# Sorted-block attention and a token/channel MLP on one core: plain second product in three batches, block products in the last, other slots for the token layer

## The chip, the core and the metric

The kernel runs on one NeuronCore of a Trainium2 chip. Five engines work side by side, each in its own program order: TensorE (PE, matmuls into PSUM), VectorE (DVE), ScalarE (ACT), GpSimd (POOL) and SyncE (SP, which here only starts transfers). Sixteen DMA engines move data. The metric is the time of one execution on the device in microseconds; lower is better. Inputs and output lie in the device's main memory in float32.

## The reference

Attention over sorted blocks, then a token-mixing layer and a feed-forward layer (FFN). Cut to what matters:

```python
# q, k, v: (4, 8, 768, 64); sort_net: (4, 8, 8, 8); blocks of 96 rows
P = sort_net
for _ in range(5):                       # row and column normalisation
    P = exp(P - P.max(-1)); P = P / P.sum(-1); P = P / P.sum(-2)
k_sorted = einsum('bhij,bhjcd->bhicd', P, k_blocks)
v_sorted = einsum('bhij,bhjcd->bhicd', P, v_blocks)
attn = softmax(q_blocks @ k_sorted.T / sqrt(64)) @ v_sorted   # within a block
x = attn.transpose(0, 2, 1, 3).reshape(4, 768, 512)
a1 = alpha1 * x + beta1
u  = x + lam * einsum('ts,bsd->btd', w_tok, a1)               # token layer
a2 = alpha2 * u + beta2
out = u + lam * (relu(a2 @ w_ch1) @ w_ch2)                    # w_ch1 512 x 2048, w_ch2 2048 x 512
```

## The kernel before

Everything runs in one program, with the order of each engine written out by hand. After a start of some 36 us (sorting weights, batch 0's attention, weights loaded) the body is a walk over four batches b and, in each, three pairs g of token tiles (128 tokens each, so 256 per pair). For each pair (b, g) come:

- eight h units ("h", 0 to 7; `h_unit`): 8 matmuls of 256 columns each into a PSUM tile h_ps, 64 in a pair; ScalarE applies relu into hT (`h_part`).
- the product steps ("c", n): the second FFN product of the pair, from hT and W2p.

The work of the next batch is hung into numbered places of this walk: `put(b, g, kind, n, ...)` files it, `run` emits it right after h unit or product step n of pair (b, g). So a place sets where an instruction stands in the order of every engine that it uses, TensorE, VectorE, ScalarE, and the queues of SP and POOL.

Two forms of the second product exist. `ch_plain` (line 842): for each of the two token tiles, 16 matmuls of 512 columns into one PSUM tile ch_ps, four per step, eight steps; then VectorE multiplies by lam while it empties the PSUM tile, POOL adds u, SP stores. `ch_step` (line 787), the block form: the product is cut into 2 x 2 blocks and made with seven block products instead of eight (`product`), 7 x 8 = 56 matmuls of 256 columns into cha_ps and chb_ps. It needs four sums of blocks of hT per pair (`sums`, tile hs, eight VectorE operations), differences of blocks of W2p made once (`weights`, tiles T23 and T4, and one block of W2p overwritten), and several copies and adds on ScalarE and VectorE to put the four result blocks together. Before, pair (0, 0) is plain and the eleven others are in block form; the weight differences are made in pairs (0, 0) and (0, 1).

The hung-in work of batch b, in the pairs of batch b - 1 and the first ones of b:

- `load_kv`, `load_q`: POOL starts the loads of v, k (tile raw) and q (tile qn). The load of batch 3 is behind `gate` (line 201), a POOL copy that reads one element of uT of pair (1, 1), so it waits until that transposition has landed.
- `mix_matrix` (the sorting matrix spread over partitions, VectorE), `mix_v` and `mix_k` (matmuls that sort v and k; the results leave PSUM as mixed and kT), `bounce_v` and `back_v` (SP writes mixed to device memory, vscr, and reads it back in the layout of the tile Vs).
- q is turned: for batch 1 by TensorE (`q_turn_late`, line 511, qt_ps to qT), for batches 2 and 3 by transposing transfers of SP (`q_cross`).
- `score` (sc_ps, then exp on ScalarE) and `pv` (value products x_ps, then VectorE divides into x), 8 each per batch, through two PSUM slots psA that mix_ps and kmix_ps use too.
- `half_done` (line 953): VectorE moves tails of x between partitions and makes a half of a1, the operand a of the token layer.
- `moe_tok`: the token layer of one token tile, six matmuls of 512 columns into tok_ps; VectorE makes u from it, ScalarE a float16 copy. `moe_cross`: two transposing transfers of SP make uT of a pair. `moe_affine`: four VectorE operations make a2T, the input of the pair's h units.

h_ps, tok_ps, ch_ps, cha_ps, chb_ps and qt_ps go in turn through four PSUM slots (psB): a tile waits until the fourth tile before it has been emptied. Of u there are seven tiles, of ost (the output of a token tile) two.

Line 69 is the helper that records every engine instruction, so groups in the profile are told apart by their tiles.

Of the kernel before, what the change touches and what calls it, by code (L numbers as in the profile page):

```python
# [7 lines left out]
FT = mybir.dt.float32  # L8
F16 = mybir.dt.float16
BF = mybir.dt.bfloat16  # L10
AF = mybir.ActivationFunctionType
ALU = mybir.AluOpType
# [4 lines left out]
def kernel(  # L17
# [22 lines left out]
    B, H, S, D = q.shape  # L40
    NB = sort_net.shape[-1]
    BLK = S // NB
    C = H * D
    HID = moe_w_ch1.shape[1]
    NT = S // 128
    CT = C // 128
    HT = HID // 128
    BH = B * H
    HB = BLK // 2
    H4 = H // 2  # L50
    GRP = D + 2
    TAIL = 6 * BLK
    NG = NT // 2
    GS = 256
    HP = HT // 2
# [21 lines left out]
    pe = Engine(nc.tensor)  # L77
    dve = Engine(nc.vector)
    act = Engine(nc.scalar)
# [14 lines left out]
    def psb(shape, dtype, name):  # L94
        return pools["psB"].tile(shape, dtype, name=name, tag="psB")
# [92 lines left out]
    qn_of = {}  # L188

    gate = const([1, 1], F16, "gate")  # L190

    def load_q(b):
        qn_of[b] = att.tile([128, NT, H, D], F16, name="qn", tag="qn", bufs=1)
        for kt in range(NT):
            pool.dma_start(
                qn_of[b][:, kt, :, :], q[b, :, kt * 128:(kt + 1) * 128, :].rearrange("h p d -> p h d"),
            )
# [171 lines left out]
    def mix_matrix(b):  # L369
        mix_values(b, psa)  # L370
        big = att.tile([128, 2, H * NB], F16, name="bigM", tag="bigM", bufs=3)
        dve.tensor_tensor(
            big[:], bigV[b][:].rearrange("p h i -> p (h i)").unsqueeze(1).to_broadcast([128, 2, H * NB]),
            mth[:].unsqueeze(2).to_broadcast([128, 2, H * NB]), ALU.mult,
        )
        bigM[b] = big
        bgp = att.tile([128, 2, 2, H4, NB], F16, name="bigP", tag="bigP", bufs=3)
        for th in range(2):
            dve.tensor_tensor(
                bgp[:, :, th, :, :], bigV[b][:].rearrange("p (g a) i -> p a g i", a=2),  # L380
                mth[:, th:th + 1].unsqueeze(2).unsqueeze(3).to_broadcast([128, 2, H4, NB]), ALU.mult,
            )
        bigP[b] = bgp
# [127 lines left out]
    def q_turn_late(b, g, eng):  # L511
        if g == 0:
            qT_of[b] = att.tile([128, H4, S], F16, name="qT", tag="qT", bufs=1)
        ps = psb([128, S], F16, "qt_ps")
        for kt in range(NT):
            pe.transpose(
                ps[:, kt * 128:(kt + 1) * 128],
                qn_of[b][:, kt, 2 * g:2 * g + 2, :].rearrange("p a d -> p (a d)"), ident16[:],
            )
        eng(qT_of[b][:, g, :], ps[:])  # L520

    mixed = {}

# [161 lines left out]
    def moe_tok(b, kt, ps):  # L685
        tok_part(b, kt, 0, C, ps)
        if b not in u16_of:
            u16_of[b] = moep.tile([128, NT, C], F16, name="u16", tag="u16", bufs=1)
        u = u_tile(b, kt)
        dve.scalar_tensor_tensor(u, tok_of[(b, kt)][:], 1.0 / LIFT, x_of[b][:, kt, :], op0=ALU.mult, op1=ALU.add)  # L690
        act.copy(u16_of[b][:, kt, :], u)

    def moe_cross(b, g):
        uT = uT_of[(b, g)] = att.tile([128, CT, GS], F16, name="uT", tag="uT", bufs=2)
        for m in range(2):
            sp.dma_start_transpose(
                uT[:, :, m * 128:(m + 1) * 128], u16_of[b][:, 2 * g + m, :],
            )

    def moe_affine(b, g):  # L700
        for ci in range(CT):
            affine(b, g, ci, uT_of[(b, g)][:, ci, :], dve)
# [26 lines left out]
    def block(b, g, r, c):  # L729
        return hT_of[(b, g)][:, :, c, r * 128:(r + 1) * 128]  # L730
# [16 lines left out]
    def weights(n):  # L747
        B = [[W2p[:, r * HP:(r + 1) * HP, c * CH:(c + 1) * CH] for c in range(2)] for r in range(2)]
        if n == 0:
            T23.append(moep.tile([128, 2, HP, CH], F16, name="T23", tag="t23", bufs=1))  # L750
            T4.append(moep.tile([128, HP, CH], F16, name="T4", tag="t4", bufs=1))
            dve.tensor_tensor(T23[0][:, 1], B[1][1], B[0][1], ALU.subtract)
        elif n == 1:
            dve.tensor_tensor(T23[0][:, 0], T23[0][:, 1], B[0][0], ALU.add)
        elif n == 2:
            dve.tensor_tensor(T4[0][:], B[1][0], T23[0][:, 0], ALU.subtract)
        else:
            dve.tensor_tensor(B[0][1], B[0][1], B[0][0], ALU.subtract)
# [20 lines left out]
    def store(b, kt, ost, c, tail_q):  # L779
        sp.dma_start(out[b, kt * 96:(kt + 1) * 96, c], ost[0:96, c])  # L780
        tail_q(out[b, TAIL + kt * 32:TAIL + (kt + 1) * 32, c], ost[96:128, c])
# [59 lines left out]

    def ch_plain(b, g, n):
        kt = 2 * g + n // 4
        if n % 4 == 0:
            ch_of[0] = psb([128, C], FT, "ch_ps")
        cps = ch_of[0]
        for m in range(4 * (n % 4), 4 * (n % 4) + 4):
            pe.matmul(
                cps[:], block(b, g, n // 4, m // HP)[:, m % HP, :], W2p[:, m, :],
                start=(m == 0), stop=(m == HT - 1),  # L850
            )
        if n % 4 == 3:
            ost = att.tile([128, C], FT, name="ost", tag="ost", bufs=2)
            dve.tensor_tensor(ost[:], cps[:], lamB[:], ALU.mult)
            pool.tensor_tensor(ost[:], ost[:], u_of[(b, kt)][:], ALU.add)
            store(b, kt, ost, all_c, act_out)

    copy = dve.tensor_copy

# [64 lines left out]
    def put(b, hf, kind, n, *todo):  # L924
        at.setdefault((b, hf, kind, n), []).extend(todo)
# [17 lines left out]
    put(0, 0, "c", 3, lambda: moe_tok(0, 5, psb), lambda: moe_cross(0, 2))  # L943
    put(0, 0, "c", 5, lambda: moe_affine(0, 1))
    put(0, 1, "c", 1, lambda: moe_affine(0, 2))
    for n, at_ in enumerate(((0, "c", 7), (1, "h", 0), (1, "h", 1), (1, "h", 2))):
        put(0, *at_, lambda n=n: weights(n))
    put(1, 0, "h", 4, lambda: mix_matrix(3))

    def attn(b, kind, n):  # L950
        return (lambda: score(b, n // 2, n % 2, psa)) if kind == "s" else (lambda: pv(b, n // 2, n % 2))
# [25 lines left out]
    for b in range(1, B):  # L977
        p = b - 1
        if b > 1:
            for n, at_ in enumerate(((2, "h", 1), (2, "h", 3), (2, "h", 5))):  # L980
                put(p - 1, *at_, lambda b=b, n=n: mix_v(b, n, act.copy))
            put(p - 1, 2, "h", 7, lambda b=b: bounce_v(b))
            put(p - 1, 2, "c", 6, lambda b=b: back_v(b))
            for n in range(3):
                at_ = ((p - 1, 2, "c", 4), (p - 1, 2, "c", 6), (p, 0, "h", 1)) if b == 2 else (
                    (p - 1, 1, "c", 6), (p - 1, 2, "c", 4), (p - 1, 2, "c", 6)
                )
                put(*at_[n], lambda b=b, n=n: mix_k(b, n, (both[n == 2],) * 4))
            for kt in range(NT):
                at_ = (1, "c", 1) if b == 3 else (2, "h", 0) if kt < 3 else (2, "c", 0)  # L990
                put(p - 1, *at_, lambda b=b, kt=kt: q_cross(b, kt))
            if b + 1 < B:
                put(p, 0, "c", 0, lambda b=b: load_kv(b + 1), lambda b=b: load_q(b + 1))
            for what, at_ in (
                ("s0", (0, "h", 5)), ("s2", (0, "c", 1)), ("p0", (0, "c", 3)), ("s4", (0, "c", 5)), ("p2", (1, "h", 1)),
                ("s6", (1, "h", 3)), ("p4", (1, "c", 1)), ("p6", (1, "c", 3)),
            ):
                for i in range(2):
                    put(p, at_[0], at_[1], at_[2] + (i if what == "p6" else 0), attn(b, what[0], int(what[1]) + i))
            put(p, 1, "h", 2, half_done(b, 0))  # L1000
        put(p, *((1, "c", 6) if b == 1 else (2, "h", 0)), half_done(b, 1))
        put(p, 2, "h", 5, lambda b=b: moe_tok(b, 0, psb))
        put(p, 2, "h", 6, lambda b=b: moe_tok(b, 1, psb), lambda b=b: moe_cross(b, 0))
        put(p, 2, "c", 4, lambda b=b: moe_affine(b, 0))
        put(b, 0, "h", 0, lambda b=b: moe_tok(b, 2, psb))
        put(b, 0, "h", 2, lambda b=b: moe_tok(b, 3, psb), lambda b=b: moe_cross(b, 1))
        put(b, 0, "h", 5, lambda b=b: moe_tok(b, 4, psb))
        put(b, 0, "h", 7, lambda b=b: moe_tok(b, 5, psb), lambda b=b: moe_cross(b, 2))
        put(b, 0, "c", 4, lambda b=b: moe_affine(b, 1))
        put(b, 1, "c", 2, lambda b=b: moe_affine(b, 2))  # L1010

# [12 lines left out]
    for b in range(B):  # L1024
        for g in range(NG):
            for j in range(HP):
                if b or g or j > 2:
                    h_unit(b, g, j)
                    if j == 4 and (b or g):
                        sums(b, g, 0, 4, range(4))  # L1030
                    run(b, g, "h", j)
            for n in range(7 if b or g else 8):
                (ch_step if b or g else ch_plain)(b, g, n)
                run(b, g, "c", n)


# [28 lines left out]
```

## Time and profile before

| | |
|---|---|
| time, median of 13 runs | 271.24 us (269.39 to 276.16) |
| the profiled execution | 272.33 us, its span 270.5 us |
| mean granted clock of TensorE | 0.982 |
| matmuls of the h units | 768 of 128 x 256 |
| block products cha_ps, chb_ps | 352 and 264 of 128 x 256, in eleven pairs |
| plain product ch_ps | 32 of 128 x 512, in pair (0, 0) |
| VectorE hs (sums of blocks) | 44 + 22 + 22 operations, 0.42 us each |
| ScalarE copies out of cha_ps | 33 of 0.372 us |
| POOL ost + u | 22 of 1.336 us |
| Vs read back (Vs<-vscr) | 3 transfers, 7.8 to 9.0 us to landing |
| uT transpositions | 22, median 2.5 us to landing, longest 11.7 |
| loads of q (qn) | 18 of 128 KB, median 12.6 us to landing |

How to read it: a line of the timeline is a merged run of equal instructions with its start, the time from its first start to its last end, and, in brackets, how long the engine had stood idle before and what ended that. The recorded durations of matmuls overlap, so the pace of TensorE is read from starts. The DMA row of the page shows the transfer engines busy without a break from about 7 to 88 us, and little used after 150.

### The profile page before, as it was taken

What the parts mean: (1) busy time and instruction counts of PE and PEld (TensorE: products, weight loads), DVE (VectorE), ACT (ScalarE), POOL (GpSimd) and SP (SyncE); (2) the same over time, 40 slices, a digit from 0 to 9 for tenths busy, and PEclk for the clock granted to TensorE, in tenths of its full rate; (3) what the DMA queues carried; (4) which work ended last, traced back from release to release, by engine and by line L of the source; (5) the groups of instructions that cost most, each with busy time, mean ns of one, the idle gap of its engine ahead of it and who ended that gap; (6) DMA issues with size and microseconds to landing.
All of it is one profiled execution on the core that took longest, in us unless ns stands there. A gap on an engine that the chain in (4) does not pass through costs nothing.

```text
span 270.5 us, 6546 instructions
## 1 busy us (share of the span) xinstructions
PE 250.4 (93%) x2665; PEld 191.1 (71%) x2665; DVE 190.3 (70%) x433; ACT 147.5 (55%) x264; POOL 77.8 (29%) x94
## 2 busy tenths in 40 slices
PE   7986999999699889999999999999997999999992
PEld 3464776547488648767888678678896687788881
DVE  5768667779759945774989957647899574545554
ACT  3666575158654734948563956575725325444440
POOL 8791953314620300306610303001103020030300
PEclk9999999999889979999999999999999999999997
DMA  6999999999999265696999224970202104210202
GB/s 102 194 208 196 206 207 214 190 208 162 188 195 61 57 97 117 159 137 109 190 172 140 79 52 122 157 91 10 80 2 78 39 10 109 42 52 29 64 22 72
DMA packets 68078, 31.25 MB, mean 116 GB/s; under 512 B 57216, under 2 KB 63888, under 8 KB 68048
## 3 DMA queue, kind: packets, MB, share of 16 engines
q0 software_dynamic: 26352, 15.34, 43.0%
q1 hardware_dynamic: 41504, 15.36, 31.6%
q8 instruction: 21, 0.34, 0.5%
q10 hardware_dynamic: 192, 0.13, 0.2%
q14 instruction: 9, 0.07, 0.1%
HBM read 32.78 MB, written 8.65 MB: 153 GB/s over the span
## 4 chain that ended last, share of the span: by engine, by line
PE 58%; DVE 21%; DMA 9%; issue 4%; ACT 4%; POOL 2%; SPq 1%; ACTq 0%; DVEq 0%; POOLq 0%
PE h_ps L69 18%; PE cha_ps L69 11%; PE tok_ps L69 10%; PE chb_ps L69 8%; DVE ost L69 6%; DVE a L69 4%; DVE x L69 4%; DMA Vs<-vscr 3%; DMA v<-in_v_dram 3%; PE x_ps L69 3%; DVE kT L69 2%; DMA out_dram<-ost 2%; PE sc_ps L69 2%; PE v_ps L69 2%; DVE a2T L69 1%
## 5 line engine op out<-in xcount | busy, mean ns | idle before, releaser
L69 PE MATMUL h_ps<-a2T,W1p 128*128 128x256 bf16 x768 | 94.8, 276 | 0.5 <-DVE a2T L69 0.3
L69 PEld LDWEIGHTS <-W1p 128*128 128x128 bf16 x768 | 74.8, 99 | 14.8 <-issue 1.3
L69 ACT ACTIVATE hT<-h_ps 128x512 f16<-128x512 f32 x96 | 55.9, 601 | 26.8 <-PE h_ps L69 22.6
L69 POOL TENSOR_TENSOR ost<-ost,u 128x512 f32<-128x512 f32 x22 | 29.3, 1336 | 143.0 <-DVE ost L69 113.3
L69 PEld LDWEIGHTS <-hs 128*128 128x128 f16 x352 | 33.5, 98 | 4.9 <-issue 0.4
L69 PE MATMUL tok_ps<-a,w_tokT 128*128 128x512 f16 x132 | 32.6, 383 | 4.2 <-DVE a L69 4.1
L69 ACT CAST u<-u 128x512 f16<-128x512 f32 x22 | 13.6, 619 | 37.3 <-DVE u L69 37.3
L69 PEld LDWEIGHTS <-hT 128*128 128x128 f16 x296 | 28.1, 98 | 7.3 <-ACT hT L69 0.7
L69 DVE SCALAR_TENSOR_TENSOR u<-tok_ps,x 128x512 f32<-128x512 f32 x22 | 15.2, 692 | 21.7 <-PE tok_ps L69 18.9
L69 DVE TENSOR_TENSOR hs<-hT 128x512 f16<-128x512 f16 x44 | 18.5, 420 | 16.3 <-ACT hT L69 16.3
L69 ACT ACTIVATE et<-sc_ps 96x768 f16<-96x768 f32 (+1 forms) x32 | 24.8, 808 | 7.9 <-PE sc_ps L69 7.9
L69 PEld LDWEIGHTS <-w_tokT 128*128 128x128 f16 x132 | 12.8, 99 | 16.8 <-DVE a L69 5.0
L69 ACT COPY ost<-cha_ps 128x256 f32<-128x256 f32 x33 | 12.3, 372 | 22.2 <-PE cha_ps L69 19.6
L69 PE MATMUL cha_ps<-T,hs 128*128 128x256 f16 x176 | 22.8, 272 | 0.1
L69 PE MATMUL chb_ps<-W2p,hs 128*128 128x256 f16 x176 | 22.8, 273 | 0.0
L69 POOL DMA_DIRECT2D qn<-in_q_dram x18 | 16.0, 909 | 14.2 <-DMA raw<-in_v_dram 7.2
L69 ACT CAST kT<-kmix_ps 64x512 f16<-64x512 f32 x24 | 17.3, 720 | 3.0 <-PE kmix_ps L69 2.7
L69 DVE TENSOR_TENSOR ost<-ost,lamB 128x256 f32<-128x256 f32 (+1 forms) x23 | 18.3, 796 | 0.4
L69 PE MATMUL x_ps<-Vs,et 96*128 96x65 f16 (+4 forms) x288 | 13.4, 196 | 4.2 <-DMA Vs<-vscr 2.7
L69 DVE TENSOR_TENSOR ost<-ost,chb_ps 128x256 f32<-128x256 f32 x22 | 9.2, 418 | 11.3 <-PE chb_ps L69 10.4
L69 DVE TENSOR_TENSOR x<-x_ps,rcb 96x512 f16<-96x512 f32 x24 | 16.5, 686 | 0.8
L69 PEld LDWEIGHTS <-et 96*128 96x128 f16 (+4 forms) x288 | 12.4, 101 | 6.0 <-issue 4.0
(131 smaller groups left out, 323.5 us busy)
## 6 DMA issues: line engine op xcount, KB each, us to landing
out_dram<-ost SPq DMA_DIRECT2D x22, 192.0 KB, 2.2
raw<-in_v_dram POOLq DMA_DIRECT2D x6, 384.0 KB, 8.4
raw<-in_k_dram POOLq DMA_DIRECT2D x6, 384.0 KB, 11.8
qn<-in_q_dram POOLq DMA_DIRECT2D x18, 128.0 KB, 12.6
vscr<-mixed SPq DMA_DIRECT2D x6, 384.0 KB, 5.3
Vs<-vscr SPq DMA_DIRECT2D x3, 768.0 KB, 8.4
W1p<-in_moe_w_ch_dram POOLq DMA_DIRECT2D x4, 512.0 KB, 13.6
W2p<-in_moe_w_ch_dram POOLq DMA_DIRECT2D x4, 512.0 KB, 14.1
```

What stands on the lines that cost most here:

```text
L69: ins = getattr(self.eng, name)(*args, **kwargs)
```

## The change

1. A pair is in block form only in the last batch (`by_blocks`): pairs (0, 1) to (2, 2) use the plain form. The weight differences move from pairs (0, 0) and (0, 1) to pair (2, 2). `mix_matrix(3)` moves from pair (1, 0) to pair (0, 0).
2. The q of batch 1 is loaded in four transfers instead of six, in which a partition gets six rows that follow each other (1536 bytes in device memory); TensorE turns it with 12 transposes of 64 columns per two heads instead of 6 of 128, and the copy out of PSUM writes with a stride of six elements.
3. The token tiles of a batch move: of the six, the first two one h unit later, the third and fourth from pair (b, 0) to product steps 4 and 5 of the pair before, the last two to h units 2 and 3 of pair (b, 0). Their transposing transfers move with them.
4. The last value products move: p4 and p5 from product step 1 to h unit 6 of the second pair, p6 and p7 one product step earlier.
5. `ch_plain` gets a branch for the last token tile of all; with `by_blocks` as it is, it is not reached.

```diff
     def load_q(b):
+        if b == 1:
+            qn_of[b] = att.tile([128, H, NT, D], F16, name="qn", tag="qn", bufs=1)
+            for g in range(H4):
+                pool.dma_start(
+                    qn_of[b][:, 2 * g:2 * g + 2, :, :],
+                    q[b, 2 * g:2 * g + 2].rearrange("h (p t) d -> p h t d", t=NT),
+                )
+            return
...
         ps = psb([128, S], F16, "qt_ps")
-        for kt in range(NT):
-            pe.transpose(
-                ps[:, kt * 128:(kt + 1) * 128],
-                qn_of[b][:, kt, 2 * g:2 * g + 2, :].rearrange("p a d -> p (a d)"), ident16[:],
-            )
-        eng(qT_of[b][:, g, :], ps[:])
+        for t in range(NT):
+            for h2 in range(2):
+                pe.transpose(
+                    ps[h2 * 64:h2 * 64 + 64, t * 128:(t + 1) * 128], qn_of[b][:, 2 * g + h2, t, :], ident16[:],
+                )
+        eng(
+            qT_of[b][:, g, :].rearrange("p (r t) -> p r t", t=NT),
+            ps[:].rearrange("p (t r) -> p r t", t=NT),
+        )
...
+    def by_blocks(b, g):
+        return b == B - 1
...
-    for n, at_ in enumerate(((0, "c", 7), (1, "h", 0), (1, "h", 1), (1, "h", 2))):
-        put(0, *at_, lambda n=n: weights(n))
-    put(1, 0, "h", 4, lambda: mix_matrix(3))
+    for n, at_ in enumerate(((2, 2, "h", 3), (2, 2, "h", 5), (2, 2, "c", 2), (2, 2, "c", 7))):
+        put(*at_, lambda n=n: weights(n))
+    put(0, 0, "c", 7, lambda: mix_matrix(3))
...
-                ("s6", (1, "h", 3)), ("p4", (1, "c", 1)), ("p6", (1, "c", 3)),
+                ("s6", (1, "h", 3)), ("p4", (1, "h", 6)), ("p6", (1, "c", 2)),
...
-        put(p, 2, "h", 5, lambda b=b: moe_tok(b, 0, psb))
-        put(p, 2, "h", 6, lambda b=b: moe_tok(b, 1, psb), lambda b=b: moe_cross(b, 0))
-        put(p, 2, "c", 4, lambda b=b: moe_affine(b, 0))
-        put(b, 0, "h", 0, lambda b=b: moe_tok(b, 2, psb))
-        put(b, 0, "h", 2, lambda b=b: moe_tok(b, 3, psb), lambda b=b: moe_cross(b, 1))
-        put(b, 0, "h", 5, lambda b=b: moe_tok(b, 4, psb))
-        put(b, 0, "h", 7, lambda b=b: moe_tok(b, 5, psb), lambda b=b: moe_cross(b, 2))
+        put(p, 2, "h", 6, lambda b=b: moe_tok(b, 0, psb))
+        put(p, 2, "h", 7, lambda b=b: moe_tok(b, 1, psb), lambda b=b: moe_cross(b, 0))
+        put(p, 2, "c", 4, lambda b=b: moe_affine(b, 0), lambda b=b: moe_tok(b, 2, psb))
+        put(p, 2, "c", 5, lambda b=b: moe_tok(b, 3, psb), lambda b=b: moe_cross(b, 1))
+        put(b, 0, "h", 2, lambda b=b: moe_tok(b, 4, psb))
+        put(b, 0, "h", 3, lambda b=b: moe_tok(b, 5, psb), lambda b=b: moe_cross(b, 2))
...
-                    if j == 4 and (b or g):
+                    if j == 4 and by_blocks(b, g):
                         sums(b, g, 0, 4, range(4))
...
-            for n in range(7 if b or g else 8):
-                (ch_step if b or g else ch_plain)(b, g, n)
+            for n in range(7 if by_blocks(b, g) else 8):
+                (ch_step if by_blocks(b, g) else ch_plain)(b, g, n)
```

More of the change, by code (lines that the diff above doesn't have):

```diff
@@ L843, in ch_plain @@
         kt = 2 * g + n // 4
+        split = (b, kt) == (B - 1, NT - 1)
         if n % 4 == 0:
@@ L848, in ch_plain @@
             pe.matmul(
-                cps[:], block(b, g, n // 4, m // HP)[:, m % HP, :], W2p[:, m, :],
-                start=(m == 0), stop=(m == HT - 1),
-            )
-        if n % 4 == 3:
+                cps[:, lo_c if split else all_c], block(b, g, n // 4, m // HP)[:, m % HP, :],
+                W2p[:, m, lo_c if split else all_c], start=(m == 0), stop=(m == HT - 1),
+            )
+        if n % 4 < 3:
+            return
+        if not split:
             ost = att.tile([128, C], FT, name="ost", tag="ost", bufs=2)
             dve.tensor_tensor(ost[:], cps[:], lamB[:], ALU.mult)
-            pool.tensor_tensor(ost[:], ost[:], u_of[(b, kt)][:], ALU.add)
+            (dve if (b, g) == (B - 1, NG - 1) else pool).tensor_tensor(ost[:], ost[:], u_of[(b, kt)][:], ALU.add)
             store(b, kt, ost, all_c, act_out)
+            return
+        for c in (lo_c, hi_c):
+            if c is hi_c:
+                cps = psb([128, C], FT, "ch_ps")
+                for m in range(HT):
+                    pe.matmul(
+                        cps[:, c], block(b, g, 1, m // HP)[:, m % HP, :], W2p[:, m, c],
+                        start=(m == 0), stop=(m == HT - 1),
+                    )
+            ost = att.tile([128, C], FT, name="ost", tag="ost", bufs=2)
+            dve.tensor_tensor(ost[:, c], cps[:, c], lamB[:, c], ALU.mult)
+            dve.tensor_tensor(ost[:, c], ost[:, c], u_of[(b, kt)][:, c], ALU.add)
+            store(b, kt, ost, c, act.dma_start)
+    def by_blocks(b, g):
+        return b == B - 1
     copy = dve.tensor_copy
```

## The prediction

> **What bounds the kernel now.** I read the page first: busy shares, the clock row, the chain that ended last.
>
> ```profile
> span 270.5 us, 6546 instructions
> ...
> PE 250.4 (93%) x2665; PEld 191.1 (71%) x2665; DVE 190.3 (70%) x433; ACT 147.5 (55%) x264; POOL 77.8 (29%) x94
> ...
> PEclk9999999999889979999999999999999999999997
> ...
> PE 58%; DVE 21%; DMA 9%; issue 4%; ACT 4%; POOL 2%; SPq 1%; ACTq 0%; DVEq 0%; POOLq 0%
> ```
>
> TensorE is busy nearly always, and its clock dips near slices 11 and 14. Next the timeline of TensorE, for the price of a matmul and every wait in brackets.
>
> ```profile
> 50.90 1.02 PE L69 MATMUL ch_ps<-W2p,hT 128*128 128x512 f16 x4
> 51.76 1.46 PE L69 MATMUL tok_ps<-a,w_tokT 128*128 128x512 f16 x6
> ...
> 68.94 1.05 PE L69 MATMUL h_ps<-a2T,W1p 128*128 128x256 bf16 x8
> 72.68 0.44 PE L69 MATMUL x_ps<-Vs,et 96*128 96x65 f16 x8 [2.70 <-DMA Vs<-vscr]
> ...
> 73.48 1.89 PE L69 MATMUL h_ps<-a2T,W1p 128*128 128x256 bf16 x8
> ...
> 95.88 1.85 PE L69 MATMUL tok_ps<-a,w_tokT 128*128 128x512 f16 x6 [2.17 <-DVE a L69]
> ...
> 98.37 1.91 PE L69 MATMUL h_ps<-a2T,W1p 128*128 128x256 bf16 x8
> ...
> 209.39 1.47 PE L69 MATMUL tok_ps<-a,w_tokT 128*128 128x512 f16 x6 [1.64 <-DVE a L69]
> ...
> 238.58 7.15 PE L69 MATMUL h_ps<-a2T,W1p 128*128 128x256 bf16 x64
> 245.57 0.93 PE L69 MATMUL cha_ps<-W2p,hT 128*128 128x256 f16 x7
> ...
> 251.80 7.15 PE L69 MATMUL h_ps<-a2T,W1p 128*128 128x256 bf16 x64
> ```
>
> Starts give the true price, since durations overlap. 64 matmuls of 256 columns take 245.57 - 238.58 = 6.99 us, 0.109 each. Four of 512 columns take 51.76 - 50.90 = 0.86, 0.2157 each. A block pair takes 251.80 - 245.57 = 6.23 for 56 matmuls. There are three real waits (start to start 2.86, 2.33, 1.80), and after the first two come matmuls at half speed (eight in about 1.8 instead of 0.87): the granted clock is 0.5 for 3.41 us from 73.5 and from 97.4, costing 1.7 each. After the wait at 209 it stays at 1.0. Summing, over the matmuls from 36 us on, the distance to the next start less the median of its shape gives 20.2 us of loss. VectorE is what keeps TensorE waiting twice:
>
> ```profile
> 85.75 0.96 DVE L69 TENSOR_TENSOR a<-x,alphaB 128x1536 f16<-128x1536 f16 x1
> ...
> 91.97 1.86 DVE L69 COPY x<-x 32x512 f16<-32x512 f16 x3
> 93.87 0.96 DVE L69 TENSOR_TENSOR a<-x,alphaB 128x1536 f16<-128x1536 f16 x1
> ```
>
> The second half of the token operand comes behind some 3 us of output sums.
>
> **The change part by part.** *Plain product.* Eight pairs, (0,1) to (2,2), go from 56 matmuls of 256 columns to 32 of 512: 32 x 0.2157 = 6.90 against 56 x 0.109 = 6.10, +0.80 each, **+6.4**. Certain, since TensorE sets the pace there.
>
> *What the block form cost besides columns.* In the product stages of those eight pairs the same start-to-start sum loses 1.11, 0.27, 0.45, 0.51, 0.27, 0.45, 0.06 and 0.27 = 3.4 us on sums not ready and slots not free. A plain pair waits only for the last hT, which has 7 x 0.2157 = 1.5 us for a 0.60 activation. I leave 0.1 per pair: **-2.6**. VectorE sheds, per pair, eight sums of 0.42 and five or six output operations (0.4 to 0.9), and gains two evictions of 0.68: about 5 us. ScalarE sheds four copies of 0.37.
>
> *The token wait of batch 3* (1.80 at 207.6). Its operand is made at the head of pair (2,2): eviction 0.7, tails 0.9 to 1.9, two products 0.96, so 3.6 to 4.6 after the last product matmul. The token matmuls now follow seven h units (6.1) instead of six. Gone, as is batch 2's at 153.5 (0.5): **-2.3**. The weight differences (1.2, 2.2, 1.2 and 1.2 on VectorE) come behind it in pair (2,2), where VectorE otherwise has only evictions; batch 3 reads them some 15 us later.
>
> *The token wait of batch 1.* I walk the queues of pair (0,1) from the first value product. TensorE, with h 0.873, product step 0.863, value product 0.25, scores 0.28: the fourth h unit of pair (0,2) could start at 15.9, its token matmuls at 20.3. VectorE: the sixth x ends at 8.9; then half_done 2.8, eviction 0.6, two x of 0.84, half_done 2.8, and only then the eviction of the second product tile, done at 17.5. psB has four slots, and that fourth h unit takes the one of this tile. So the wait does not vanish: it becomes one for ch_ps, about 1.5 (0 if I overstate VectorE, 2.5 if the tails take 1.86 again): **-0.8**. At 1.5 it is shorter than the 1.80 that left the clock alone: **-1.7**.
>
> *The value wait* (2.86 at 69.8). Vs<-vscr is issued at 63.58 behind two transposes (1.2 each) and an output store whose issue took 1.9 while the 6144 short packets of q of batch 1 were draining (to 60.5). With 1024 long ones instead they should end near 56, estimated from the rate of the 1024-byte packets (195 per us). Store, transposes and bounce then go up to 1.5 earlier. TensorE arrives about 0.5 later, since the copy of q through VectorE writes with a stride. Bounds: wait 0.9 to 2.9; I take 1.2, **-1.7**, and the slow clock goes with it, **-1.7**. If SP gains nothing, both stay.
>
> *q by six-row runs.* 48 transposes of half width replace 24. No row shows a half-width transpose of 128 rows. Below: nothing, as six matmuls into separate column strips (rr_ps) took 0.40 where one takes 0.28; above: 24 x 0.056 = 1.3. Two strided copies on VectorE cost up to 0.4 more each. I take **+0.4**, being nearer to rr_ps.
>
> *Token layer in other slots.* Six tiles as before, none added. Two now use psB beside the product tile; they and kT of ScalarE leave hT 0.8 us of room. On SP the second pair of transposes now goes ahead of Vs<-vscr. Vs of batch 2 is issued some 13.4 us after the product of pair (0,2) begins; its first reader comes at 25.0; uncontended it takes 7.8. But see the slower rival: **+0.5**. The small waits of the h stages of (1,0) and (2,0), 1.02 and 0.70, lose their VectorE half: **-0.7**.
>
> Sum: 6.4 - 2.6 - 2.3 - 0.8 - 1.7 - 1.7 - 1.7 + 0.4 + 0.5 - 0.7 = **-4.2 us**. The profiled execution is 272.33 (span 270.5), 1.09 above the median of 271.24; from the median that gives **267.0**.
>
> The Trainium skill, "TensorE: Matmul & The Clock Gate", section "Why this matters for your kernels", lets the clock fall for idle gaps of some 3 us and more. The gaps of 2.2 and 2.7 here were followed by half clock, so the row decides; by the rule those drops had another cause, 3.4 would not come back, and the sum would be -0.8.
>
> **Rivals.** *Slower: the load of batch 3 runs into Vs of batch 2* (chance 0.2). POOL's gate waits for uT(1,1), today until 123.7, after Vs has landed (waits view: POOL gate 10.8). With the transposes ahead of Vs, the gate opens about 1.3 us after Vs is issued, and four 384 KB loads and six of q start against it. For it: uT transposes that shared the engines with running loads took 11.7 us to land (issued at 125.35), against a median of 2.5; and Vs of batch 1, with a load 2.7 us behind it, took 8.97. Against: there the load's first packets only came when Vs was nearly through. It decides from a landing over 11.6 us after issue. At 18: 6.4 of wait and 1.7 of clock, in place of my 0.5: -4.2 + 7.6 = +3.4, **274.6**. The Trainium skill, "DMA: Bandwidth & Descriptors", section "Queues, rings and completion order", has each engine go round between queue rows packet by packet. By that rule alone the load would share from its first packet, not from the end of Vs, and this rival would be the forecast.
>
> *No change: waits only move* (0.16). Vs still waits 2.9, ch_ps 2.3, both followed by half clock. Of the sum 6.4 - 2.6 - 2.3 - 0.7 + 0.4 remain, +1.2: **272.4**. For it: VectorE's queue in pair (0,1) is still about 1.5 us too long. Against: both must be as bad as today.
>
> *All waits gone* (0.13): the slot wait too (1.5), Vs fully (1.2), no collision (0.5), half of the rest: -8, **263.2**. It needs VectorE 1.5 us ahead of my walk.
>
> **How the numbers follow.** The forecast holds 0.51, its own range 265 to 269.5. The whole range takes in the waits-only-move case and the milder end of the collision, and most of the waits-gone case: 263.5 to 274. About 0.5% (1.36 us) is what a measurement can tell from no change. Faster: 0.47 of the forecast and 0.13 = 0.60. Same: 0.04 and 0.11 = 0.15. Slower: 0.20 and 0.05 = 0.25.
>
> **What would show it.** Product stages near 6.9 us plus attention; no wait for a; a wait for DVE ost of 1 to 2 us at the fourth h unit of pair (0,2); Vs<-vscr issued before 62.5; no clock of 0.5 past 70 us. It is wrong if x_ps of batch 2 waits for Vs, or if ch_ps matmuls stand at more than 0.22 each.

## The result and the profile after

The changed kernel takes 275.52 us (median of 11 runs, 274.01 to 279.38), the kernel before 271.03 (median of 48 runs in the same comparison, 268.01 to 276.16). The ratio is 1.0188 (95% interval 1.0157 to 1.0219): the change made the kernel slower by 1.6 to 2.2%. The ratio compares fast executions alone (some executions of a kernel run longer, at a lower granted clock), so it is a little above the quotient of the two medians. The forecast was 267.0, the range 263.5 to 274.0. The time is close to that of the slower rival, 274.6.

The page after, with the rows that answer to those shown of before:

```profile
span 273.6 us, 6041 instructions
...
PE 254.3 (93%) x2497; PEld 171.8 (63%) x2497; DVE 154.1 (56%) x337; ACT 136.5 (50%) x232; POOL 75.4 (28%) x92
...
PEclk9999999999999999996899999999999999999998
...
PE 76%; DMA 9%; ACT 5%; DVE 5%; POOL 2%; issue 1%; ACTq 0%; DVEq 0%; POOLq 0%
```

VectorE does 36 us less (154.1 against 190.3) and has nearly left the chain that ended last (5% against 21%). The two dips of the clock (slices 11 and 12, and slice 15, counted from 1) are gone, and there is one new, deeper dip in slices 19 and 20. The waits view, TensorE alone, from 36 to 260 us (who waited for whom, total us, times, longest), says how few waits are left:

```profile
PE x_ps L69 <- DMA Vs<-vscr: 6.7, 1, 6.7
PE x_ps L69 <- ACT hT L69: 1.0, 1, 1.0
PE kmix_ps L69 <- ACT kT L69: 0.7, 1, 0.7
PE h_ps L69 <- ACT qT L69: 0.4, 1, 0.4
```

Before, the same view had three waits for DVE a (4.1 in all) and one for Vs of batch 1 (2.7). All three for a are gone. The 1.0 put down to hT is what is left of the wait for Vs of batch 1: it ended 0.14 us after Vs had landed, the same distance as before. What is new is one wait of 6.7 us. The timeline of TensorE shows where it lies, in the product stage of pair (1, 0):

```profile
116.81 1.89 PE L69 MATMUL ch_ps<-W2p,hT 128*128 128x512 f16 x8
118.64 0.51 PE L69 MATMUL sc_ps<-qT,kT 64*128 64x96 f16 x16
119.08 1.90 PE L69 MATMUL ch_ps<-W2p,hT 128*128 128x512 f16 x8
127.67 1.11 PE L69 MATMUL x_ps<-Vs,et 96*128 96x65 f16 x16 [6.69 <-DMA Vs<-vscr]
128.60 3.60 PE L69 MATMUL ch_ps<-W2p,hT 128*128 128x512 f16 x8
132.13 0.53 PE L69 MATMUL sc_ps<-qT,kT 64*128 64x96 f16 x16
132.59 1.90 PE L69 MATMUL ch_ps<-W2p,hT 128*128 128x512 f16 x8
134.33 1.91 PE L69 MATMUL h_ps<-a2T,W1p 128*128 128x256 bf16 x16
```

The first value products of batch 2 need Vs. The eight ch_ps matmuls behind them take 3.6 where the eight ahead take 1.9: the half clock has followed the wait. The queues of SP (first fence) and POOL (second) say why Vs is late:

```profile
107.68 2.51 SPq L69 DMA_TRANSPOSE uT<-u  x2
110.29 0.53 SPq L69 DMA_DIRECT2D Vs<-vscr  x1
```

```profile
111.48 0.18 POOL L69 COPY gate<-uT 1x1 f16<-1x1 f16 x1 [3.10 <-DMA uT<-u]
111.98 1.10 POOL L69 DMA_DIRECT2D raw<-in_v_dram  x2 [0.32 <-PE h_ps L69]
```

The transposition that the gate reads now goes ahead of Vs on SP. So the gate opens 1.2 us after Vs is issued, and the load of batch 3 starts 1.7 after it. Before, Vs was issued first and the transpositions behind it (SP in the first fence), and the gate opened ten us after Vs (POOL in the second):

```profile
113.76 0.38 SPq L69 DMA_DIRECT2D Vs<-vscr  x1
114.63 12.00 SPq L69 DMA_TRANSPOSE uT<-u  x4
```

```profile
123.70 0.18 POOL L69 COPY gate<-uT 1x1 f16<-1x1 f16 x1 [10.84 <-DMA uT<-u]
```

After the change, the chain of waits has one piece of transfer:

```profile
110.29 17.34 DMA Vs<-vscr
...
127.67 1.11 PE x_ps L69 x16
```

Vs took 17.34 us to land. Before, the view gives 9.0 for batch 1 and 7.8 for batch 3; for batch 2 it gives no landing, but the packets were through 7.7 us after the issue.

### The profile page after: what moved, and what is told of

Same layout as the page of the kernel before. It is cut to its first block, busy times and chain, and to the rows that moved or that the text cites. A ratio compares the mean times of both kernels' runs of the same rounds, so it can differ in the third digit from the quotient of the medians.

```text
span 273.6 us, 6041 instructions
## 1 busy us (share of the span) xinstructions
PE 254.3 (93%) x2497; PEld 171.8 (63%) x2497; DVE 154.1 (56%) x337; ACT 136.5 (50%) x232; POOL 75.4 (28%) x92
## 4 chain that ended last, share of the span: by engine, by line
PE 76%; DMA 9%; ACT 5%; DVE 5%; POOL 2%; issue 1%; ACTq 0%; DVEq 0%; POOLq 0%
PE h_ps L69 27%; PE ch_ps L69 21%; PE tok_ps L69 11%; DMA Vs<-vscr 6%; PE x_ps L69 4%; PE cha_ps L69 4%; DMA v<-in_v_dram 3%; PE chb_ps L69 3%; ACT kT L69 2%; PE sc_ps L69 2%; DVE a L69 2%; PE v_ps L69 2%; PE mix_ps L69 1%; ACT et L69 1%; PE kmix_ps L69 1%
## 5 line engine op out<-in xcount | busy, mean ns | idle before, releaser
L69 PE MATMUL h_ps<-a2T,W1p 128*128 128x256 bf16 x768 | 92.4, 273 | 0.6 <-ACT qT L69 0.4
L69 PE MATMUL ch_ps<-W2p,hT 128*128 128x512 f16 x288 | 70.5, 386 | 0.0
L69 PEld LDWEIGHTS <-hT 128*128 128x128 f16 x360 | 34.0, 99 | 29.5 <-issue 1.7
L69 DVE TENSOR_TENSOR ost<-ch_ps,lamB 128x512 f32<-128x512 f32 x18 | 12.4, 690 | 33.9 <-PE ch_ps L69 24.9
L69 POOL DMA_DIRECT2D qn<-in_q_dram x16 | 13.5, 855 | 16.9 <-DMA raw<-in_v_dram 8.6
L69 DVE RECIPROCAL rcb<-x_ps 96x8 f32<-96x8 f32 x24 | 4.8, 199 | 20.6 <-PE x_ps L69 20.6
L69 DVE TENSOR_SCALAR a2T<-uT,ab2col 128x256 bf16<-128x256 f16 x44 | 14.6, 394 | 0.6 <-DMA uT<-u 0.5
L69 PE MATMUL warm_ps<-wz 128*128 128x512 f16 x30 | 9.8, 474 | 1.2 <-DVE wz L69 1.2
L69 DVE TENSOR_TENSOR hs<-hT 128x512 f16<-128x512 f16 x12 | 5.1, 422 | 9.8 <-ACT hT L69 9.8
L69 DVE CAST kT<-kmix_ps 64x512 f16<-64x512 f32 x12 | 8.6, 713 | 3.2 <-PE kmix_ps L69 3.1
## 6 DMA issues: line engine op xcount, KB each, us to landing
raw<-in_v_dram POOLq DMA_DIRECT2D x6, 384.0 KB, 10.8
W1p<-in_moe_w_ch_dram POOLq DMA_DIRECT2D x4, 512.0 KB, 13.4
```

The costliest lines, as they stand in the source:

```text
L69: ins = getattr(self.eng, name)(*args, **kwargs)
```

## The experiments

Theory A: the load of batch 3, let off early by the gate, slows Vs of batch 2, and this is the whole loss. The rivals: B, the new order of the work, above all the plain product, is itself slower, and the wait is only the place where it shows; C, Vs is late for another reason on SP, and the load only happens to run beside it. (The expectations below call C "rival A".)

**The gate on Vs** (the changed kernel, one line).

```diff
         if b == 3:
-            pool.tensor_copy(gate[:], uT_of[(1, 1)][0:1, 0, 255:256])
+            pool.tensor_copy(gate[:], Vs[0:1, 0, 0:1])
```

> The changed kernel, but the gate before the load of batch 3 reads an element of Vs (so the load starts only when Vs of batch 2 has landed) instead of one of uT(1,1). Theory (the load shares the DMA engines with Vs<-vscr and holds it up): Vs is issued near 110 as before and lands about 8 us later, x_ps of batch 2 no longer waits (6.7 us in the changed kernel) and the half clock behind it (1.9 us) goes: about 8.8 us less than the changed kernel, some 266.5 us, ratio to before 0.98 to 0.99. Rival A (Vs is late because SP issues it late, the load is innocent): x_ps waits 5 us or more, 274 to 276 us. Rival B (the plain product's 6.4 us of columns is the loss, another wait takes the place): 271 to 275 us.

Measured: 266.94 us, ratio to the kernel before 0.988 (0.976 to 1.0), span 265.0. The timelines of POOL and, below, of TensorE:

```profile
118.68 0.18 POOL L69 COPY gate<-Vs 1x1 f16<-1x1 f16 x1 [9.83 <-DMA Vs<-vscr]
119.19 1.09 POOL L69 DMA_DIRECT2D raw<-in_v_dram  x2 [0.32 <-issue]
```

```profile
117.12 1.89 PE L69 MATMUL ch_ps<-W2p,hT 128*128 128x512 f16 x8
...
119.39 1.90 PE L69 MATMUL ch_ps<-W2p,hT 128*128 128x512 f16 x8
121.13 0.68 PE L69 MATMUL x_ps<-Vs,et 96*128 96x65 f16 x16
121.64 1.89 PE L69 MATMUL ch_ps<-W2p,hT 128*128 128x512 f16 x8
...
125.76 1.91 PE L69 MATMUL h_ps<-a2T,W1p 128*128 128x256 bf16 x16
```

Vs is issued at 110.05, within 0.3 us of its place after the change, and the gate that reads it opens at 118.68, so it landed within 8.6 us. The value products start without a wait, and the eight ch_ps behind them take 1.9. One line takes 8.6 us off. That speaks for A, against B, since everything else of the change is still there, and against C, since SP's order is untouched.

**Vs first on SP** (the changed kernel, the gate as it was).

```diff
-            put(p - 1, 2, "c", 6, lambda b=b: back_v(b))
+            put(p - 1, 2, "c", 4 if b == 2 else 6, lambda b=b: back_v(b))
```

> The changed kernel, but for batch 2 alone SP is given Vs<-vscr (back_v) after product step 4 of pair (0,2), ahead of the transposes of uT(1,1), as in the kernel before; the gate is as in the changed kernel, and so opens after Vs, since the transposes queue behind it. Theory: Vs issued near 107, landing in about 8 us, no wait of x_ps, 265 to 268 us like the gate on Vs. Rival A: the same, as Vs is earlier. Rival B: 271 to 275 us.

Measured: 266.76 us, ratio 0.988 (0.978 to 0.997), span 264.7. SP, then POOL:

```profile
107.77 0.32 SPq L69 DMA_DIRECT2D Vs<-vscr  x1
108.15 8.13 SPq L69 DMA_TRANSPOSE uT<-u  x2
```

```profile
117.86 0.18 POOL L69 COPY gate<-uT 1x1 f16<-1x1 f16 x1 [9.42 <-DMA uT<-u]
```

With Vs ahead of the two transpositions, these take 8 us to issue behind it, and the old gate opens only at 117.86, when Vs is in (it landed 9.1 us after its issue). The same time comes back without a touch on the gate. As Vs is also issued 2.5 us earlier, this run alone would not exclude C, but the gate on Vs did. So it is the order of Vs and these two transpositions on SP that lets the load off early.

**The kernel before without its gate.** If A holds, the kernel before must be hurt in the same way when its load is let off early.

```diff
-        if b == 3:
-            pool.tensor_copy(gate[:], uT_of[(1, 1)][0:1, 0, 255:256])
```

> The kernel before without the gate: the load of batch 3 starts when its buffers are free, near 113, where Vs of batch 2 is issued at 113.8. Theory: Vs takes 13 us or more to land instead of 8, x_ps of batch 2 (127.7 in before) waits 0 to 6 us, with up to 3.4 us of half clock behind it: 272 to 279 us. Rival A and rival B: no change, within 0.5% of 271 us.

Measured: 281.74 us, ratio 1.040 (1.026 to 1.055). The chain of waits:

```profile
113.74 21.99 DMA Vs<-vscr
...
135.78 1.11 PE x_ps L69 x16
```

The load starts 1.0 us ahead of Vs here, Vs takes 22 us, and the value products wait 7.9, both more than expected. The price is 11 us without any plain product or new slot in the kernel: A again, and B cannot say it.

**The parts alone, on the kernel before.** First the plain product in batches 0 to 2, with the weight differences in pair (2, 2):

```diff
-    for n, at_ in enumerate(((0, "c", 7), (1, "h", 0), (1, "h", 1), (1, "h", 2))):
-        put(0, *at_, lambda n=n: weights(n))
+    for n, at_ in enumerate(((2, 2, "h", 3), (2, 2, "h", 5), (2, 2, "c", 2), (2, 2, "c", 7))):
+        put(*at_, lambda n=n: weights(n))
...
-            for n in range(7 if b or g else 8):
-                (ch_step if b or g else ch_plain)(b, g, n)
+            for n in range(7 if b == B - 1 else 8):
+                (ch_step if b == B - 1 else ch_plain)(b, g, n)
```

> The kernel before with the plain product in batches 0 to 2 and the weight differences in pair (2,2), all else (slots, q, gate) as before. Theory: columns +6.4, waits inside the block product -2.6, the token wait of batch 3 and the small ones -2 or so, Vs of batch 2 untouched: 270 to 274 us, no wait of x_ps for Vs in batch 2. Rival B (the plain product is the loss): 275 us or more.

Measured: 269.17 us, ratio 0.995 (0.990 to 1.001), a little under the range expected. In the profiled execution (271.48 us, above the median) the three waits for a are gone too; Vs of batch 1 is still waited for (2.1), Vs of batch 2 not at all.

Then the new slots of the token layer and of the last value products alone (parts 3 and 4 of the diff of the change):

> The kernel before with the new slots of the token layer and of the last value products alone (block products, weights, q and gate as before). Theory (it is the new order on SP, transposes of uT(1,1) ahead of Vs<-vscr, that opens the gate too early): the load of batch 3 starts 1 to 2 us after Vs of batch 2, Vs takes 15 to 19 us to land, x_ps of batch 2 waits 2 to 6 us and half clock follows: 273 to 279 us, slower than before. Rival (the plain product makes the collision, by pulling the reader forward): within 0.5% of before or faster.

Measured: 275.04 us, ratio 1.016 (1.008 to 1.024). SP, POOL and TensorE:

```profile
111.14 3.23 SPq L69 DMA_TRANSPOSE uT<-u  x2
...
115.56 0.38 SPq L69 DMA_DIRECT2D Vs<-vscr  x1
```

```profile
115.70 0.18 POOL L69 COPY gate<-uT 1x1 f16<-1x1 f16 x1 [3.33 <-DMA uT<-u]
```

```profile
133.61 1.11 PE L69 MATMUL x_ps<-Vs,et 96*128 96x65 f16 x16 [7.57 <-DMA Vs<-vscr]
```

The slots alone bring the whole collision: the gate opens 0.1 us after Vs is issued, and Vs takes 18.0. The wait is longer than the 2 to 6 us expected. The product is in block form throughout, so neither the plain product nor q has a part in it.

Then q of batch 1 in six-row runs alone (part 2):

> The kernel before with q of batch 1 in six-row runs alone. Theory: it only brings Vs of batch 1 forward, by about 1 us, so the wait of x_ps in batch 1 falls from 2.7 to 1.5 to 2 us, and the half clock behind it (1.7 us) may go; transposes cost nothing that shows: 268 to 271 us. Rival (the gain at that wait came from the plain product, not from q): no change, within 0.5% of before.

Measured: 270.22 us, ratio 0.996 (0.992 to 1.001), which fits both expectations. The wait for Vs of batch 1 falls from 2.70 to 1.27, but not because Vs is early: it is issued at 63.83 (before 63.58) and lands in 8.4 instead of 9.0. TensorE comes later, for mix_ps waits 0.9 for raw, and by the start-to-start sum the product stage of pair (0, 0) loses 1.2 more than before, the h stage of (0, 1) 2.5 less. What is saved is about the half clock behind the wait, which is gone.

**Block products, with the collision mended.** Two versions between the kernels: blocks from batch 1 on (in the kernel with the gate on Vs, the weight differences in pair (0, 2)), and blocks in eleven pairs as before, with the new slots, q by runs and the gate on Vs.

```diff
     def by_blocks(b, g):
-        return b == B - 1
+        return b >= 1
...
-    for n, at_ in enumerate(((2, 2, "h", 3), (2, 2, "h", 5), (2, 2, "c", 2), (2, 2, "c", 7))):
+    for n, at_ in enumerate(((0, 2, "h", 3), (0, 2, "h", 5), (0, 2, "c", 2), (0, 2, "c", 7))):
```

> The changed kernel with the gate on Vs, and block products from batch 1 on (weight differences in pair (0,2)), plain in the three pairs of batch 0. Theory: six pairs get 0.6 us each back, the waits that the block form brought in pair (1,2) and (2,2) stay away since the token matmuls stand an h unit later: 262 to 265 us. Rival (VectorE becomes the bound again: hs, sums and weights): 266 to 270 us with waits of TensorE on DVE a or DVE ost.

Measured: 266.96 us, ratio 0.983 (0.971 to 0.994): outside the range expected and inside that of the rival, though not by a wait for VectorE. A new wait of 1.8 for ACT ost comes in pair (1, 1), and that copy of ScalarE had itself waited 2.5 for an output store; half clock follows the wait.

> The kernel before (block products in eleven pairs, weights as before) with the new slots, q in six-row runs and the gate on Vs. Theory: no collision; the two pairs (0,1) and (0,2) gain columns but VectorE's queue in (0,1) brings back a wait for DVE a of 1 to 3 us in pair (0,2): 263 to 268 us. Rival (block products are what costs, whatever the slots): 270 us or more.

Measured: 266.46 us, ratio 0.984 (0.977 to 0.991). The wait for DVE a is back, but with 0.9 us only.

Since these intervals overlap that of the mended kernel, the last and the mended kernel were run again side by side, in more rounds, with one more kernel that asks which part of the load does the harm: q at the old gate, raw behind Vs.

```diff
         if b == 3:
             pool.tensor_copy(gate[:], uT_of[(1, 1)][0:1, 0, 255:256])
+            load_q(3)
+            pool.tensor_copy(gate[:], Vs[0:1, 0, 0:1])
...
-                put(p, 0, "c", 0, lambda b=b: load_kv(b + 1), lambda b=b: load_q(b + 1))
+                put(p, 0, "c", 0, lambda b=b: load_kv(b + 1), lambda b=b: b < 2 and load_q(b + 1))
```

> The changed kernel, with the loads of batch 3 taken apart: the six loads of q (6144 packets of 128 bytes) go at the old gate, some 1.5 us after Vs of batch 2 is issued; the four raw loads (6144-byte packets) wait until Vs has landed. If it is the size of the packets that starves Vs: beside 128-byte packets it keeps one packet in two, lands 9 to 12 us after its issue, x_ps waits under 0.7 us, no half clock there, span 264.5 to 266.5, time 266 to 268. If any load that starts beside Vs keeps it from ending: landing 15 to 19, wait 5 to 8, time 272 to 276.

Measured: 267.89 us, ratio 0.991 (0.987 to 0.995). The chain of waits, then TensorE:

```profile
110.60 11.18 DMA Vs<-vscr
```

```profile
121.82 0.69 PE L69 MATMUL x_ps<-Vs,et 96*128 96x65 f16 x16 [0.76 <-DMA Vs<-vscr]
```

Landing in 11.2 and a span of 265.6 are as expected for packet size, the wait is 0.06 over its bound. With q beside Vs the value products wait 0.8 us; with the raw loads as well it is 6.7.

> The kernel before (block products in eleven pairs) with the new slots, q of batch 1 by runs, and the gate of batch 3 on Vs. Here to be set beside the next kernel on the same chip, which is the same but for the form of the product in batches 0 to 2. If the plain product is worth what my terms gave it (6.4 dearer in columns, 2.6 + 2.3 + some of the others given back by waits, most of which the slots remove as well), this one is faster by 0 to 4 us: 263 to 267. If the waits of the block form still cost what its columns save, the two are within 0.7 us of each other.

> The changed kernel with the gate of batch 3 on Vs, once more, for an interval beside the kernel of the run before it: 265.5 to 267.5, faster than the kernel before by 1 to 2%. If the collision were not all of what went wrong, it would stay above 269.

Measured: blocks in eleven pairs 266.64 us, ratio 0.987 (0.981 to 0.993), span 264.9; plain in batches 0 to 2, 267.35 us, ratio 0.989 (0.984 to 0.993), span 265.5. The two are 0.7 us apart, at the very bound that was set, and the intervals (3 and 2.4 us wide) cannot tell them apart. Their waits on TensorE can be told: in block form (only its largest are shown)

```profile
PE cha_ps L69 <- ACT ost L69: 1.6, 1, 1.6
PE x_ps L69 <- DMA Vs<-vscr: 1.3, 1, 1.3
PE tok_ps L69 <- DVE a L69: 0.9, 1, 0.9
PE kmix_ps L69 <- ACT kT L69: 0.7, 1, 0.7
```

against the plain form, in which the wait for Vs of batch 1 is the longest:

```profile
PE x_ps L69 <- DMA Vs<-vscr: 1.2, 1, 1.2
PE mix_ps L69 <- DMA raw<-in_v_dram: 0.8, 1, 0.8
PE kmix_ps L69 <- ACT kT L69: 0.7, 1, 0.7
PE h_ps L69 <- ACT qT L69: 0.4, 1, 0.4
```

By the start-to-start sum of the prediction the block form loses 14.8 us on TensorE from 36 us on, the plain one 9.3: 5.5 less, for 6.4 more in columns. So the form of the product is nearly a draw by the profiles, and all mended versions are some 1 to 1.7% faster than the kernel before.

## Why the prediction was wrong

The step that failed is the term for Vs of batch 2, "+0.5", in the part on the token layer's slots. The prediction saw the mechanism, priced it as the slower rival, and gave it a chance of 0.2. Measured by starts, the product stage of pair (1, 0) takes 134.33 - 116.81 = 17.52 after the change and 125.76 - 117.12 = 8.64 with the gate on Vs: +8.9, of which 6.85 is the wait (8.59 from the second run of ch_ps to x_ps, where 1.74 is the pace) and 2.0 the half clock. The rival had 6.4 + 1.7 = 8.1, from a landing of 18; it was 17.34, but Vs was issued 14.6 us into pair (0, 2)'s product (13.4 in the walk) with its reader ready at 25.1, so that a landing of 10.5, not 11.6, was the bound.

The argument that kept the rival small was that the first packets of the load behind Vs of batch 1 came only when Vs was nearly through. That held in the changed kernel as well: of the 6144 packets of Vs, 5618 had moved when the first long packet of the load came, at 116.4. But "nearly through" is no landing. By 116.8 there were 5900; the last 244 took until 127.2. With the gate on Vs the last 244 take 1.4 us, and the whole Vs is moved in 6.8. With the slots alone the argument did not even hold: the first long packet came at 118.1, after 1949 packets of Vs, and the landing was 18.0 all the same, with only 1.3 us for the last 244. In both kernels Vs landed only when 9 in 10 of the load's 256 long packets had moved (by 124.7 and 127.1), so how much of Vs was left when they came, 526 packets or 4195, made little difference to the landing. The row that spoke for the rival should have weighed more: the uT transposes that took 11.7 us beside running loads instead of 2.5 are small transfers too.

The other steps, one by one, with the losses on TensorE by the start-to-start sum, before and with the gate on Vs (where the collision does not hide them):

| step | predicted | before | mended | measured |
|---|---|---|---|---|
| columns of the plain product | +6.4 | | | 20 ch_ps in 4.32 us: 0.216 each, as assumed |
| product stages, eight pairs | -2.6 | 3.4 | 1.7 | -1.7 |
| token wait, batches 2 and 3 | -2.3 | 2.35 | 0.0 | -2.3 |
| token wait of batch 1 with its clock | -2.5 | 4.0 | 0.0 | -4.0 |
| value wait with its clock, q's turn | -3.0 | 5.9 | 3.0 | -2.9 |
| small waits of (1,0) and (2,0) | -0.7 | 1.7 | 0.45 | -1.3 |
| all after 36 us | -11.1 | 20.2 | 8.6 | -11.6 |

That the total of the predicted losses comes so near is partly luck: the product stages gave back 0.9 less than predicted, the token wait of batch 1 gave back 1.5 more. The rows add up to -12.2; the product stage of pair (0, 0), which no step named, loses 0.6 more than before.

*Product stages.* Five of eight pairs lose nothing; (0, 1), (1, 0) and (2, 0), where value products and scores stand in between, still lose 0.6 each instead of the 0.1 that was left them.

*Token wait of batch 1.* The predicted wait for the slot of ch_ps at the fourth h unit of pair (0, 2) did not come. The walk through VectorE's queue was nearly right: the second product tile was to be emptied 17.5 after the first value product, and was 89.4 - 71.3 = 18.1 after it. The timeline of VectorE after the change:

```profile
88.72 0.68 DVE L69 TENSOR_TENSOR ost<-ch_ps,lamB 128x512 f32<-128x512 f32 x1
```

And that of TensorE:

```profile
84.82 1.91 PE L69 MATMUL h_ps<-a2T,W1p 128*128 128x256 bf16 x16
...
87.00 1.91 PE L69 MATMUL h_ps<-a2T,W1p 128*128 128x256 bf16 x16
```

The third and fourth h units start at 87.00 and, 0.87 later, 87.87, without a gap, while that tile is emptied only from 88.72 on. So the fourth unit had another slot: the four slots do not go strictly in turn, though the part on the kernel before says so. The step "that fourth h unit takes the one of this tile" was wrong, to the good by 1.5.

*Value wait.* The size was right, the reason only in part. Vs of batch 1 was issued at 62.67 after the change (predicted: before 62.5). With q alone it was issued no earlier than before, and SP took as long from the first bounce to Vs (7.34 us, before 7.35), so the 128-byte packets of q were not what held SP back. Nor did the long packets of q end near 56: it was 59.5 with q alone and 58.3 after the change (before: 60.8). After the change the wait is 1.0, and no half clock follows it. (The half clock of the kernel before lasted 3.41 us each time, as read, but from 72.95 and 96.84, half a us earlier than the prediction has it.)

*q by runs.* From the first of twelve half-width transposes to the next instruction it is 0.46 us (61.23 to 61.69), from the first of six full ones before 0.34 (61.73 to 62.07). Four times 0.12 is +0.5, against +0.4 predicted.

So without the collision the sum of the rest was -4.7. The spans give 265.0 and 265.5 against 270.5, so -5.0 to -5.5; but the profiled execution of before is 1.3 above its median, and by the ratio, 0.989 (0.984 to 0.993), it is -3.1 (-4.3 to -1.9). With the collision's 8.9 on top, that makes +5.8 by the ratio and +3.4 to +3.9 by the spans; measured are +5.1 and +3.1.

Nor do the parts add up: alone, the plain product gives -0.5% and q -0.4%, neither clear of nothing, and slots and q with the gate on Vs -1.3%, where the plain product adds nothing that can be told. The plain product removes the waits for a, and the slots alone all but 0.9 us of them.

How two transfers share the engines shows most plainly in the kernel before without its gate: the transfer view from 125 to 132 us, while q (queue q0) and Vs (queue q1), both of 128-byte packets, run together (queue, packets, MB, share of the engines):

```profile
q0 software_dynamic: 3984, 0.50, 109.1%
q1 hardware_dynamic: 3982, 0.51, 91.7%
```

One packet each. The Trainium skill's rule in "DMA: Bandwidth & Descriptors", section "Queues, rings and completion order", that an engine goes round between queue rows packet by packet, agrees with these counts, and it would have made the rival the forecast.

## What to carry to other kernels

When an instruction moves past another on a queue, ask what else waits for the moved one: here a gate read a transposition that the change put ahead of the transfer which the gate was to protect. Tie a gate to the transfer that it protects, not to something that happens to land later. And when a rival's price is known and its only defence is that a competitor starts "nearly" too late, price what is left: here 526 of 6144 packets were left, an estimate of 13 us at the 40 per us that Vs had beside long packets in the kernel without its gate; they took 10.8, until the long packets were through.

## What the runs showed of the hardware

A transfer of short packets is held up by the length of the packets beside it. The transfer views of the changed kernel from 118 to 124 us and of the kernel with q at the old gate from 118 to 121, in turn:

```profile
q0 software_dynamic: 228, 1.11, 92.9%
q1 hardware_dynamic: 250, 0.19, 21.0%
```

```profile
DMA packets 3444, 0.43 MB, mean 145 GB/s; under 512 B 3444, under 2 KB 3444, under 8 KB 3444
```

Beside raw, whose 181 packets of 6144 bytes take 0.47 us each (median), the queue of Vs moves only 250 packets in six us, 139 of them of Vs (85 of the rest are of an output store). Beside q more than 1100 short packets move per us, and Vs lands in 11.2 us instead of 17.3. In the kernel before without its gate Vs moved some 40 packets per us while raw ran (about one for each packet of the load: 187 on its queue against 203 from 118 to 123 us), then 569 beside q; with the gate on Vs it moves 900 per us. The 6144-byte packets came 4.4 us after the issue of their load (111.98, first packet 116.4); before, with Vs through, they came 1.3 after it.

One packet each does not hold in the tails: at the old gate 81 packets of Vs moved in those three us against 3363 of q. It would fit if the last packets of Vs stood on few of the engines, but the records do not name the engine, and this was not tried.

The half clock does not follow from the length of a wait alone. Waits of 2.70 and 2.17 us in the kernel before were followed by 3.4 us of half clock each, and so was the wait of 1.80 in the kernel with blocks from batch 1 on; in the kernel with q alone the same wait for a, 2.17 again, had none behind it. What decides is not shown. After 6.7 the half clock lasted some 6.8 us (from 125.4, so 4.5 of it fell on matmuls), after the waits of 7.57 and 7.89 some 10.2: one, two and three times 3.41.
